# Low parts of layer 1's weights and of the first unit's work: from GpSimd to VectorE

## The chip, the cores and the metric

The kernel runs on one core of a Trainium2 chip. The metric is device time in microseconds (us) of one execution; lower is better. A core has TensorE (PE in the profile; PEld is its weight load), VectorE (DVE), ScalarE (ACT), GpSimd (POOL) and SyncE (SP), whose queue issues nearly all DMAs. Each engine runs its own list of instructions in order, and waits on semaphores where an operand comes from another engine.

## The reference

Three steps: a scan over 768 positions, then two dense layers.

```python
def _attn_ref(q, k, v, a_re, a_im):            # (4, 8, 768, 48) each
    mag = np.sqrt(a_re * a_re + a_im * a_im)
    scale = np.minimum(mag, 0.999) / (mag + 1e-06)
    a_re_n, a_im_n = (a_re * scale, a_im * scale)
    for t in range(S):
        ar, ai = (a_re_n[:, :, t, :, None], a_im_n[:, :, t, :, None])
        new_re = ar * S_re - ai * S_im
        new_im = ar * S_im + ai * S_re
        kv = np.einsum('bhd,bhe->bhde', k[:, :, t], v[:, :, t])
        S_re, S_im = (new_re + kv, new_im)
        y[:, :, t] = np.einsum('bhd,bhde->bhe', q[:, :, t], S_re)
...
def _moe_ref(x, w_in, w_out):                   # x 3072 x 384, w_in 384 x 2048
    h = np.maximum(x @ w_in, 0.0)
    return h * h @ w_out
...
def _moe2_ref(x, w_in, w_out):
    h = x @ w_in
    g = np.where(h > 0.0, h, alpha * (np.exp(np.minimum(h, 0.0)) - 1.0))
    return g @ w_out
```

## The kernel before

The scan is done in chunks of 128 positions. A *unit* is one chunk of two of the four batches, 256 tokens in all; there are 12 (NU). For each unit `E_steps` makes the decay from logarithms, an arctan and running sums (two matmuls with a triangle of ones), with Exp and Sin on ScalarE, and from it the scaled queries and keys qn and kn (`fin`, four halves each). `P_steps` then transposes them on TensorE, multiplies them (the scores), masks the product on VectorE (amat), multiplies it with v and adds the carried state. Its output x (`xev`, and `xmove`, six small DMAs) is the input of layer 1.

Layer 1 goes by *ticks* (u, j): for unit u and each of 16 blocks j of 128 hidden columns, `moe1_gemm1` makes the hidden block (nine matmuls, the *first product*) and ScalarE applies Relu, Square and a Copy; two ticks later `moe1_gemm2` multiplies with the second weight (nine matmuls, the *second product*). The matmuls take a rounded format, so each operand is split in two: a high part (a ScalarE copy into that format) and a low part (the operand less its high part, one subtraction). Three matmuls, high by high, high by low and low by high, then stand for one.

The weights come as 64-bit numbers. `load_bits` fetches block j of both weights of a layer into one of two raw buffers (384 KB each DMA), `decode` makes 32-bit numbers of it in three VectorE steps, and `split` makes the high and the low part, wh and wl. For layer 1 the low part is made on GpSimd (line 319), as is the activation's low part glo of every unit (line 656). Layer 2's are split later with the same function, on VectorE. The table `POOL` names what GpSimd does of `E_steps` by unit, its last entry serving all units from 2 on: rho is the product of line 441 that goes into the arctan, q0, q1, k0 and k1 are halves of qn and kn (line 523), lo is the low part of line 455. In every unit from 2 on GpSimd also handles a carry (lines 479 and 480).

Steps are put into ticks by the tables `E_AT`, `P_AT` and `D_AT`; unit 0, unit 1's `E_steps` and the decoding of layer 1's weights stand in the ticks before the first product. The order on each engine is then set by a scheduler that plays the program through with its own costs, so a step that moves to another engine moves others as well. What the profile's lines are: 231 and 242 are the helpers for ScalarE; 307 to 309 the three decode steps; 313 the check of the raw bits; 392 to 395 the running sums; 414, 433, 441, 442, 488, 494, 495, 515 and 523 VectorE's part of `E_steps`; 563, 570, 587 and 596 the matmuls of `P_steps`; 573, 603 and 613 VectorE's part of it; 648 and 669 the first and second products of layer 1; 709 and 737 those of layer 2.

Of the kernel before, what the change touches and what calls it, by code (L numbers as in the profile page):

```python
# [9 lines left out]
F32 = mybir.dt.float32  # L10
F32R = mybir.dt.float32r
U32 = mybir.dt.uint32
I32 = mybir.dt.int32
ACTF = mybir.ActivationFunctionType
ALU = mybir.AluOpType
# [178 lines left out]
def fast_path(  # L194
# [15 lines left out]
    nc = tc.nc  # L210
# [16 lines left out]
    vec = nc.vector  # L227
    pe = nc.tensor

    def act(out, in_, func, **kw):  # L230
        nc.scalar.activation(out=out, in_=in_, func=func, **kw)  # L231
# [12 lines left out]
    const = ctx.enter_context(tc.tile_pool(name="const", bufs=1))  # L244
# [9 lines left out]
    def bank(i):  # L254
        return psum.tile([128, 512], F32, tag=f"b{i}", name=f"b{i}")


    ident = const.tile([128, 128], F32, name="ident")
    mask = const.tile([128, 128], F32, name="mask")
    triph = const.tile([128, 128], F32, name="triph")  # L260
    maskr = const.tile([128, 128], F32R, name="maskr")
    bias_c = const.tile([128, 4], F32, name="bias_c")
    stat = const.tile([128, 3, 2 * NU], F32, name="stat")
    ratio = const.tile([128, NU], F32, name="ratio")
# [3 lines left out]
    def setup_consts():  # L268
        g = nc.gpsimd
        g.memset(mask, 1.0)  # L270
        g.affine_select(out=mask, in_=mask, pattern=[[1, 128]], base=0, channel_multiplier=-1,
                        compare_op=ALU.is_ge, fill=0.0)
        g.affine_select(out=ident, in_=mask, pattern=[[-1, 128]], base=0, channel_multiplier=1,
                        compare_op=ALU.is_ge, fill=0.0)
        g.memset(bias_c[:, 0:1], 1e-36)
        g.memset(bias_c[:, 1:2], math.log(2e-6))
        g.memset(bias_c[:, 2:3], 0.5 * math.pi)
        g.tensor_copy(out=maskr, in_=mask)
        vec.tensor_scalar(out=triph, in0=mask, scalar1=1.0 / TWO_PI, scalar2=None, op0=ALU.mult)

    b_eps, b_w, b_q = (bias_c[:, i:i + 1] for i in range(3))
# [8 lines left out]
    def load_bits(layer, j):  # L290

        raw = raw_p.tile([128, 2, 768], U32, tag="raw", name="raw", bufs=RAW_BUFS)
        for i, which in enumerate(("in", "out")):
            nc.sync.dma_start(out=raw[:, i], in_=wbits[which, layer][j * 128:(j + 1) * 128, :])
        return raw

    def words(raw):
        two = raw.rearrange("p i (f two) -> p (i f) two", two=2)
        return two[:, :, 0], two[:, :, 1]

    def decode(raw, pinned=False):

        w0, w1 = words(raw)
        t = raw_p.tile([128, 768], F32, tag="wf", name="wf")
        f = t.bitcast(U32)
        pin = tc.keep_in_program_order if pinned else (lambda x: x)
        pin(vec.tensor_scalar(out=f, in0=w0, scalar1=29, scalar2=0xC0000000, op0=ALU.logical_shift_right, op1=ALU.bitwise_xor))  # L307
        vec.scalar_tensor_tensor(out=f, in0=w1, scalar=3, in1=f, op0=ALU.logical_shift_left, op1=ALU.bitwise_xor)
        vec.scalar_tensor_tensor(out=f, in0=w1, scalar=0x80000000, in1=f, op0=ALU.bitwise_and, op1=ALU.bitwise_xor)
        return t  # L310
# [4 lines left out]
    def split(f, j, eng):  # L315
        hi = wts.tile([128, 768], F32R, tag=f"wh{j}", name=f"wh{j}")
        lo = wts.tile([128, 768], F32R, tag=f"wl{j}", name=f"wl{j}")
        act(hi, f, ACTF.Copy)
        eng.tensor_tensor(out=lo, in0=f, in1=hi.bitcast(F32), op=ALU.subtract)
        for i, which in enumerate(("in", "out")):  # L320
            wt[which, j] = tuple(w[:, i * 384:(i + 1) * 384] for w in (hi, lo))

# [35 lines left out]
    qk = {}  # L358


    POOL = [("k0", "rho"), ("q1",), ("q0", "k0", "lo")]

    def E_steps(u):

# [14 lines left out]
        def eng(op):  # L379
            return nc.gpsimd if op in POOL[min(u, 2)] else vec  # L380

# [259 lines left out]
    def moe1_gemm1(u, j):  # L641
        hp = bank(2 + j % 2)
        wh, wl = (t.rearrange("p (k f) -> p k f", k=3) for t in wt["in", j])
        x = xs[u]
        n = 0
        for kk in range(3):
            for w, hl in ((wh, 0), (wh, 1), (wl, 0)):
                pe.matmul(out=hp[:, :UT], lhsT=w[:, kk, :], rhs=x[:, kk, hl, :], start=(n == 0), stop=(n == 8))  # L648
                n += 1
        g = moe_p.tile([128, UT], F32, tag="g", name="g")  # L650
        hi = moe_p.tile([128, UT], F32R, tag="ghi", name="ghi", bufs=GB)
        lo = moe_p.tile([128, UT], F32R, tag="glo", name="glo", bufs=GB)
        act(g, hp[:, :UT], ACTF.Relu)
        act(g, g, ACTF.Square)
        act(hi, g, ACTF.Copy)
        nc.gpsimd.tensor_tensor(out=lo, in0=g, in1=hi.bitcast(F32), op=ALU.subtract)  # L656
        g1[u, j] = (hi, lo)

    def moe1_gemm2(u, j):
# [165 lines left out]

    def piece(j):
        raw = load_bits(0, j)
        return lambda: split(decode(raw, pinned=j < 8), j, nc.gpsimd)

    def later(t, f):  # L830
        box = []
# [31 lines left out]
    load(0, ("ar", "ai"))  # L863
    nc.scalar.preload_act_table_set(LN_EXP)
    setup_consts()
    vec.memset(stat, 0.0)
    vec.memset(wbad, 0)
# [7 lines left out]
    for t in range(NT1):  # L875
        j = t - (NT1 - FT)
# [101 lines left out]
```

## Time and profile before

| | |
|---|---|
| median of 3 runs | 1084.84 us (1082.99 to 1085.36) |
| profiled execution | 1084.96 us, span 1083.2 us |
| TensorE busy | 1027.3 us (95%) |
| ScalarE busy | 712.4 us (66%) |
| VectorE busy | 615.6 us (57%) |
| GpSimd busy | 316.3 us (29%) |
| DMA | 101.38 MB, mean 94 GB/s |

The profile cuts the span into 40 slices of 27 us. TensorE's busy tenths read 2, 8, 6, 8, 7 in the first five and 9 in nearly all from there on; VectorE's read 7, 8, 8, 9, 5 in the same five and 1 to 8 later. GpSimd's work ends soon after half of the span, with layer 1. A busy figure over the whole span is a mean over these stages, so the stages are to be read apart.

### The profile page before, as it was taken

The numbers are of one execution on the slowest core, as the hardware profiler recorded it, in microseconds if no ns is written. First come the engines' busy times: TensorE is split into PE (matmuls) and PEld (weight loads), VectorE is DVE, ScalarE is ACT, GpSimd is POOL, SyncE is SP. The second block draws the span as 40 slices with busy tenths as digits, with TensorE's granted clock in tenths as the row PEclk, the third lists the DMA queues.
The fourth block names the chain that finished last, engine by engine and source line by source line (L and its number), as shares of the span: only waits on it lengthen the run. The fifth ranks groups of instructions, "written<-read, shape, count | busy, mean of one in ns | idle before, by whom it ended". The sixth has DMA issues, their size and how long they took to land.

```text
span 1083.2 us, 18914 instructions
## 1 busy us (share of the span) xinstructions
PE 1027.3 (95%) x7362; PEld 961.8 (89%) x7362; DVE 615.6 (57%) x847; ACT 712.4 (66%) x1453; POOL 316.3 (29%) x299
## 2 busy tenths in 40 slices
PE   2868799999999999999999999999999999999997
PEld 1668799999999999999999999998989999999896
DVE  7889525547394745563422134888875554554543
ACT  6666478676777767776766578666666565655553
POOL 3367345454564535453534234000000000000000
PEclk9869999999999999999999999999999999999999
DMA  7655121423253432432100044667600010000000
GB/s 233 192 170 173 38 73 37 148 81 117 69 164 116 128 137 52 146 88 97 52 16 9 16 135 151 219 210 245 215 30 30 1 59 1 5 26 1 30 1 32
DMA packets 58555, 101.38 MB, mean 94 GB/s; under 512 B 20910, under 2 KB 28590, under 8 KB 58458
## 3 DMA queue, kind: packets, MB, share of 16 engines
q1 hardware_dynamic: 58362, 100.00, 28.5%
q8 instruction: 60, 0.98, 0.4%
q14 instruction: 37, 0.30, 0.1%
q10 hardware_dynamic: 96, 0.10, 0.0%
HBM read 81.92 MB, written 15.80 MB: 90 GB/s over the span
## 4 chain that ended last, share of the span: by engine, by line
PE 45%; DMA 5%; ACT 3%; issue 2%; DVE 2%; SPq 0%; ACTq 0%; DVEq 0%
PE b L737 14%; PE b L709 13%; PE b L669 7%; PE b L648 7%; DMA raw<-in_moe_w_out_dram 3%; DMA c_x<-in_a_im_dram 2%; ACT g L231 1%; PE b L570 1%; PE b L563 1%; PE b L587 1%; PE b L589 1%; ACT e L231 1%; DVE wbad L313 0%; ACT g2h L231 0%; PE b L596 0%
## 5 line engine op out<-in xcount | busy, mean ns | idle before, releaser
L231 ACT ACTIVATE g<-b 128x256 f32<-128x256 f32 (+1 forms) x288 | 127.8, 449 | 172.0 <-PE b L648 75.7
L648 PE MATMUL b<-x,wh 128*128 128x256 f32 x1152 | 228.4, 290 | 4.6 <-DVE wf L307 4.6
L656 POOL TENSOR_TENSOR glo<-g,ghi 128x256 fp32r<-128x256 f32 x192 | 167.3, 878 | 222.0 <-ACT ghi L231 159.3
L648 PEld LDWEIGHTS b<-x,wh 128*128 128x128 f32 x1152 | 185.8, 196 | 7.0 <-issue 6.7
L648 PE MATMUL b<-x,wl 128*128 128x256 f32 x576 | 166.6, 289 | 0.0
L669 PE MATMUL b<-glo,wh 128*128 128x256 f32 x576 | 162.8, 289 | 0.6 <-POOL glo L656 0.6
L669 PE MATMUL b<-ghi,wl 128*128 128x256 f32 x576 | 159.9, 284 | 0.0
L669 PE MATMUL b<-ghi,wh 128*128 128x256 f32 x576 | 154.3, 292 | 0.5 <-ACT ghi L231 0.5
L231 ACT ACTIVATE g<-g 128x256 f32<-128x256 f32 (+1 forms) x288 | 139.0, 487 | 5.5
L737 PE MATMUL b<-wh,g2h 128*128 128x384 f32 x384 | 129.4, 337 | 0.0
L737 PE MATMUL b<-wl,g2h 128*128 128x384 f32 x384 | 129.0, 336 | 0.0
L737 PE MATMUL b<-wh,g2l 128*128 128x384 f32 x384 | 125.5, 337 | 0.7 <-DVE g2l L726 0.7
L709 PE MATMUL b<-x2l,wh 128*128 128x512 f32 x288 | 113.6, 395 | 0.0
L709 PE MATMUL b<-x2h,wl 128*128 128x512 f32 x288 | 113.6, 395 | 0.0
L648 PEld LDWEIGHTS b<-x,wl 128*128 128x128 f32 x576 | 112.9, 196 | 0.2 <-issue 0.2
L669 PEld LDWEIGHTS b<-glo,wh 128*128 128x128 f32 x576 | 110.1, 191 | 2.7 <-POOL glo L656 1.4
L709 PE MATMUL b<-x2h,wh 128*128 128x512 f32 x288 | 112.1, 389 | 0.0
L669 PEld LDWEIGHTS b<-ghi,wl 128*128 128x128 f32 x576 | 110.0, 191 | 0.3 <-issue 0.2
L669 PEld LDWEIGHTS b<-ghi,wh 128*128 128x128 f32 x576 | 104.5, 192 | 2.8 <-ACT ghi L231 0.9
L726 DVE TENSOR_TENSOR g2l<-g,g2h 128x512 fp32r<-128x512 f32 x96 | 66.6, 695 | 70.4 <-ACT g2h L231 69.8
L723 DVE SCALAR_TENSOR_TENSOR g<-e,g 128x512 f32<-128x512 f32 x96 | 66.1, 690 | 61.5 <-ACT g L231 61.5
L231 ACT ACTIVATE g2h<-g 128x512 fp32r<-128x512 f32 x96 | 60.1, 627 | 57.8 <-DVE g L724 57.5
(117 smaller groups left out, 1942.6 us busy)
## 6 DMA issues: line engine op xcount, KB each, us to landing
raw<-in_moe_w_in_dram SPq DMA_DIRECT2D x48, 384.0 KB
raw<-in_moe_w_out_dram SPq DMA_DIRECT2D x48, 384.0 KB
w2d<-wf SPq DMA_DIRECT2D x16, 384.0 KB
w<-w2d SPq DMA_DIRECT2D x8, 768.0 KB
ld_ar<-in_a_re_dram SPq DMA_DIRECT2D x12, 384.0 KB
ld_ai<-in_a_im_dram SPq DMA_DIRECT2D x12, 384.0 KB
ld_q<-in_q_dram SPq DMA_DIRECT2D x12, 384.0 KB
vt<-in_v_dram SPq DMA_DIRECT2D x12, 384.0 KB
```

The costliest lines, as they stand in the source:

```text
L231: nc.scalar.activation(out=out, in_=in_, func=func, **kw)
L563: pe.transpose(ps[0:E, i * 128:(i + 1) * 128], qk[n, u, b][:, h].rearrange("p c d -> p (c d)"), ident)
L570: pe.matmul(out=ps[:, i * 128:(i + 1) * 128], lhsT=L["k", b, g][:, i * 128:(i + 1) * 128], rhs=L["q", b, g][:, i * 128:(i + 1) * 128], sta ...
L587: pe.matmul(out=o, lhsT=vv[:, gi * D:gi * D + 64], rhs=L["a", b, g][:, i, :], start=True, stop=(c == 0))
L589: pe.matmul(out=o, lhsT=st[:, gi * D:gi * D + 64], rhs=L["q", b, g][:, i * 128:(i + 1) * 128], start=False, stop=True)
L648: pe.matmul(out=hp[:, :UT], lhsT=w[:, kk, :], rhs=x[:, kk, hl, :], start=(n == 0), stop=(n == 8))
L656: nc.gpsimd.tensor_tensor(out=lo, in0=g, in1=hi.bitcast(F32), op=ALU.subtract)
L669: pe.matmul(out=acc1[u][m], lhsT=w[:, c], rhs=g, start=(j == 0 and n == 0 and m != 1), stop=(j == FT - 1 and n == 2), skip_group_check=True)
L709: pe.matmul(out=hp, lhsT=w[:, kk, :], rhs=x[:, kk], start=(i == 0), stop=(i == 8))
L723: vec.scalar_tensor_tensor(out=g, in0=e, scalar=1.0, in1=g, op0=ALU.add, op1=ALU.mult)
L726: vec.tensor_tensor(out=lo, in0=g, in1=hi.bitcast(F32), op=ALU.subtract)
L737: pe.matmul(out=acc2[n][s][:, :DM], lhsT=g[:, t], rhs=w, start=(j == 0 and i == 0), stop=(j == FT - 1 and i == 2))
```

## The change

Three edits. The low part of layer 1's weights is subtracted on VectorE (`piece` passes vec). The low part of the activation is subtracted on VectorE for unit 0 and on GpSimd, as it was, for the others. The table POOL is empty for units 0 and 1. Besides, `split` gets a branch that would make the low part with matmuls; no caller passes pe, so it is not taken, and its constant `minus` is written once. The lines of the changed kernel stand 2 to 11 higher (L307 becomes L309, L319 becomes L330, L656 becomes L667, L515 and L523 become L526 and L534).

```diff
@@ -259,6 +259,7 @@
     mask = const.tile([128, 128], F32, name="mask")
     triph = const.tile([128, 128], F32, name="triph")
     maskr = const.tile([128, 128], F32R, name="maskr")
+    minus = const.tile([128, 128], F32R, name="minus")
     bias_c = const.tile([128, 4], F32, name="bias_c")
     stat = const.tile([128, 3, 2 * NU], F32, name="stat")
     ratio = const.tile([128, NU], F32, name="ratio")
@@ -276,6 +277,7 @@
         g.memset(bias_c[:, 1:2], math.log(2e-6))
         g.memset(bias_c[:, 2:3], 0.5 * math.pi)
         g.tensor_copy(out=maskr, in_=mask)
+        g.tensor_scalar(out=minus, in0=ident, scalar1=-1.0, scalar2=None, op0=ALU.mult)
         vec.tensor_scalar(out=triph, in0=mask, scalar1=1.0 / TWO_PI, scalar2=None, op0=ALU.mult)
 
     b_eps, b_w, b_q = (bias_c[:, i:i + 1] for i in range(3))
@@ -316,7 +318,16 @@
         hi = wts.tile([128, 768], F32R, tag=f"wh{j}", name=f"wh{j}")
         lo = wts.tile([128, 768], F32R, tag=f"wl{j}", name=f"wl{j}")
         act(hi, f, ACTF.Copy)
-        eng.tensor_tensor(out=lo, in0=f, in1=hi.bitcast(F32), op=ALU.subtract)
+        if eng is pe:
+
+            for i in range(2):
+                c = slice(i * 384, i * 384 + 384)
+                ps = bank(7)
+                pe.matmul(out=ps[:, :384], lhsT=ident, rhs=f[:, c], start=True, stop=False)
+                pe.matmul(out=ps[:, :384], lhsT=minus, rhs=hi[:, c], start=False, stop=True)
+                act(lo[:, c], ps[:, :384], ACTF.Copy)
+        else:
+            eng.tensor_tensor(out=lo, in0=f, in1=hi.bitcast(F32), op=ALU.subtract)
         for i, which in enumerate(("in", "out")):
             wt[which, j] = tuple(w[:, i * 384:(i + 1) * 384] for w in (hi, lo))
 
@@ -358,7 +369,7 @@
     qk = {}
 
 
-    POOL = [("k0", "rho"), ("q1",), ("q0", "k0", "lo")]
+    POOL = [(), (), ("q0", "k0", "lo")]
 
     def E_steps(u):
 
@@ -653,7 +664,7 @@
         act(g, hp[:, :UT], ACTF.Relu)
         act(g, g, ACTF.Square)
         act(hi, g, ACTF.Copy)
-        nc.gpsimd.tensor_tensor(out=lo, in0=g, in1=hi.bitcast(F32), op=ALU.subtract)
+        (nc.gpsimd if u else vec).tensor_tensor(out=lo, in0=g, in1=hi.bitcast(F32), op=ALU.subtract)
         g1[u, j] = (hi, lo)
 
     def moe1_gemm2(u, j):
@@ -825,7 +836,7 @@
 
     def piece(j):
         raw = load_bits(0, j)
-        return lambda: split(decode(raw, pinned=j < 8), j, nc.gpsimd)
+        return lambda: split(decode(raw, pinned=j < 8), j, vec)
 
     def later(t, f):
         box = []
```

With the edits the scheduler orders other engines' work anew. On TensorE, around the transposes of unit 1 (kernel before; b2 and b3 take the first products of unit 0, wh2 is the high part of weight 2, qn0 and kn0 are unit 1's, ident is the transposes' other operand):

```order
L648 MATMUL b3_590<-x_351,wh1_190 128x256 x2
L648 MATMUL b3_590<-x_351,wl1_191 128x256
L563 MATMUL b6_705<-ident_79,qn0_607 96x128 x4
L648 MATMUL b2_613<-x_351,wh2_206 128x256 x2
L648 MATMUL b2_613<-x_351,wl2_207 128x256
L648 MATMUL b2_613<-x_351,wh2_206 128x256 x2
L648 MATMUL b2_613<-x_351,wl2_207 128x256
L648 MATMUL b2_613<-x_351,wh2_206 128x256 x2
```

And in the changed kernel, around the same transposes (b2 and b3 now hold the first products of weights 4 and 5):

```order
L659 MATMUL b2_683<-x_353,wh4_247 128x256 x2
L659 MATMUL b2_683<-x_353,wl4_248 128x256
L659 MATMUL b3_733<-x_353,wh5_309 128x256 x2
L659 MATMUL b3_733<-x_353,wl5_310 128x256
L659 MATMUL b3_733<-x_353,wh5_309 128x256 x2
L659 MATMUL b3_733<-x_353,wl5_310 128x256
L659 MATMUL b3_733<-x_353,wh5_309 128x256 x2
L659 MATMUL b3_733<-x_353,wl5_310 128x256
L680 MATMUL b0_632<-ghi_626,wh2_208 128x256
L680 MATMUL b1_633<-ghi_626,wh2_208 128x256
L574 MATMUL b6_707<-ident_79,qn0_609 96x128 x4
```

The first transpose of unit 1 stood after the first products of weights 0 and 1; now it stands after those of weights 0 to 5, the second products of weights 0 and 1 and the first two matmuls of weight 2's.

On VectorE, the end of the weights' decoding (before; wf_551 is the last of the sixteen weights, ld_q and x1 are unit 2's, raw_2351 holds layer 2's bits, amat_879 is unit 1's):

```order
L307 TENSOR_SCALAR wf_551<-raw_516 128x768
L308 SCALAR_TENSOR_TENSOR wf_551<-raw_516,wf_551 128x768
L309 SCALAR_TENSOR_TENSOR wf_551<-raw_516,wf_551 128x768
L515 TENSOR_TENSOR ld_q_829<-ld_q_829,x2_900 128x768
L515 TENSOR_TENSOR x1_831<-x1_831,x3_901 128x768
L313 SCALAR_TENSOR_TENSOR wbad_86<-raw_2351,wbad_86 128x768
L573 TENSOR_TENSOR amat_879<-b4_874,mask_80 128x512
L603 TENSOR_TENSOR st1_92<-b5_890,tcol_526 96x384
```

And now, around the same pair of unit 2 (wl13 and wl12 are low parts of the weights):

```order
L310 SCALAR_TENSOR_TENSOR wf_533<-raw_504,wf_533 128x768
L526 TENSOR_TENSOR ld_q_831<-ld_q_831,x2_902 128x768
L526 TENSOR_TENSOR x1_833<-x1_833,x3_903 128x768
L311 SCALAR_TENSOR_TENSOR wf_533<-raw_504,wf_533 128x768
L584 TENSOR_TENSOR amat_881<-b4_876,mask_80 128x512
L614 TENSOR_TENSOR st1_93<-b5_892,tcol_528 96x384
L330 TENSOR_TENSOR wl13_512<-wf_507,wh13_511 128x768
L667 TENSOR_TENSOR glo_1074<-g_1072,ghi_1073 128x256
L330 TENSOR_TENSOR wl12_538<-wf_533,wh12_537 128x768
L499 SCALAR_TENSOR_TENSOR x6_1009<-x5_781,x4_1008 128x768
L309 TENSOR_SCALAR wf_541<-raw_515 128x768
```

The pair on ld_q and x1 and unit 1's scores amat stood behind all sixteen decodes; now they stand ahead of the last two decodes and of the last four low parts, and the check of layer 2's bits is behind them.

On SP's queue, the last loads of layer 1's weights (before; td takes unit 2's exponentials to memory, tcol fetches them back):

```order
L294 DMA raw_513<-in_moe_w_in_dram 128x768
L294 DMA raw_513<-in_moe_w_out_dram 128x768
L294 DMA raw_516<-in_moe_w_in_dram 128x768
L294 DMA raw_516<-in_moe_w_out_dram 128x768
L294 DMA raw_2351<-in_moe2_w_in_dram 128x768
L294 DMA raw_2351<-in_moe2_w_out_dram 128x768
L463 DMA td_94<-x2_900 1x768
```

And now:

```order
L296 DMA raw_504<-in_moe_w_in_dram 128x768
L296 DMA raw_504<-in_moe_w_out_dram 128x768
L474 DMA td_95<-x2_902 1x768
L296 DMA raw_515<-in_moe_w_in_dram 128x768
L296 DMA raw_515<-in_moe_w_out_dram 128x768
L478 DMA tcol_909<-td_95 48x16x1 x2
L296 DMA raw_518<-in_moe_w_in_dram 128x768
L296 DMA raw_518<-in_moe_w_out_dram 128x768
```

The loads of the last two weights (raw_515 and raw_518; raw_513 and raw_516 before) went out ahead of td; now they stand behind it, and the last one behind tcol too.

## Rows read from the trace of the kernel before

**Rows 1.** Busy time by stretch: stretch, length, busy us (instructions) per engine, clock, DMA.

```profile
57.50:80.00 22.50, 16.87 (x102) 16.29 (x102) 19.78 (x20) 16.47 (x31) 16.36 (x10) 0.65 0.50 162
80.00:114.00 34.00, 24.84 (x200) 23.45 (x200) 32.51 (x26) 20.14 (x45) 24.37 (x17) 0.95 0.48 151
114.00:138.00 24.00, 22.14 (x167) 21.49 (x164) 9.21 (x16) 13.18 (x30) 8.37 (x10) 0.86 0.17 50
138.00:300.00 162.00, 161.22 (x1451) 155.38 (x1450) 83.05 (x115) 119.78 (x267) 79.11 (x72) 1.00 0.28 87
```

**Rows 2.** TensorE's waits: who waited for whom, total us, times, longest.

```profile
PE b L587 <- DVE amat L573: 7.8, 3, 4.6
PE b L563 <- DVE qn L523: 5.4, 1, 5.4
...
PE b L563 <- ACT qT L231: 3.3, 1, 3.3
PE b L563 <- POOL qn L523: 1.9, 1, 1.9
```

**Rows 3.** Timeline of TensorE: start, us, instruction, idle time before it and releaser.

```profile
57.52 0.77 PE L648 MATMUL b<-x,wh 128*128 128x256 f32 x2 [4.59 <-DVE wf L307]
...
100.51 0.33 PE L395 MATMUL b<-x,maskr 128*128 128x384 f32 x1
...
133.83 0.64 PE L563 MATMUL b<-ident,qn 128*96 128x128 f32 x4 [1.86 <-POOL qn L523]
```

**Rows 4.** Timeline of VectorE in the opening.

```profile
12.04 0.55 DVE L307 TENSOR_SCALAR wf<-raw 128x768 uint32<-128x768 uint32 x1
...
27.72 0.54 DVE L523 TENSOR_TENSOR qn<-x,ld_q 128x384 f32<-128x384 f32 x1
28.19 0.55 DVE L523 TENSOR_TENSOR kn<-x,x 128x384 f32<-128x384 f32 x1
...
48.24 0.95 DVE L515 TENSOR_TENSOR ld_q<-ld_q,x 128x768 f32<-128x768 f32 x1
49.11 0.95 DVE L515 TENSOR_TENSOR x<-x,x 128x768 f32<-128x768 f32 x1
...
54.84 0.28 DVE L613 TENSOR_TENSOR x<-b,x 128x128 fp32r<-128x128 f32 x1
55.05 0.54 DVE L495 SCALAR_TENSOR_TENSOR x<-x,b 128x384 f32<-128x384 f32 x1
...
103.12 2.49 DVE L309 SCALAR_TENSOR_TENSOR wf<-raw,wf 128x768 uint32<-128x768 uint32 x1
105.53 0.95 DVE L515 TENSOR_TENSOR ld_q<-ld_q,x 128x768 f32<-128x768 f32 x1
106.40 5.05 DVE L515 TENSOR_TENSOR x<-x,x 128x768 f32<-128x768 f32 x1
...
112.77 0.68 DVE L573 TENSOR_TENSOR amat<-b,mask 128x512 f32<-128x512 f32 x1
113.38 0.54 DVE L603 TENSOR_TENSOR st<-b,tcol 96x384 f32<-96x384 f32 x1
```

**Rows 5.** Busy time by stretch, for the list of VectorE from its first decode.

```profile
12.04:55.35 43.31, 28.02 (x143) 19.95 (x142) 39.86 (x57) 27.55 (x48) 17.38 (x9) 0.88 0.62 192
12.04:105.61 93.57, 65.98 (x408) 56.23 (x407) 85.39 (x98) 60.35 (x115) 52.33 (x31) 0.84 0.56 180
```

**Rows 6.** Timeline of GpSimd beside the long instruction of VectorE.

```profile
106.25 1.92 POOL L480 TENSOR_TENSOR x<-x,x 1x768 f32<-1x768 f32 x1 [1.46 <-ACT x L242]
108.14 1.82 POOL L319 TENSOR_TENSOR wl<-wf,wh 128x768 fp32r<-128x768 f32 x1
```

**Rows 7.** GpSimd, 0 to 138: line, operands, count, busy us, mean ns, idle before.

```profile
L319 POOL TENSOR_TENSOR wl<-wf,wh 128x768 fp32r<-128x768 f32 x16 | 34.4, 2158 | 34.2 <-ACT wh L231 32.3 <-PE b L570 1.8
L656 POOL TENSOR_TENSOR glo<-g,ghi 128x256 fp32r<-128x256 f32 x18 | 16.9, 951 | 19.5 <-ACT ghi L231 15.9 <-issue 2.9 <-POOL glo L656 0.8
```

**Rows 8.** VectorE from 138 on: layer 2's low parts of the weights.

```profile
L319 DVE TENSOR_TENSOR wl<-w,wh 128x768 fp32r<-128x768 f32 x16 | 15.7, 979 | 15.5 <-ACT wh L231 15.3
```

## The prediction

> **What bounds the kernel now.** I read the busy time by stage first. From 138 us on, TensorE is the bound: in 138 to 300 it is busy 161.22 of 162 us [rows 1]. Before that it is not: 16.87 of 22.5, 24.84 of 34 and 22.14 of 24 us in the three stretches from 57.5 on, at a granted clock of 0.65 to 0.95. What is full there is VectorE, with 19.78 of 22.5 and 32.51 of 34 us [rows 1]. So the span is a starved opening and then TensorE at its own pace, and whatever the opening gains or loses reaches the end one for one, as long as nothing behind it begins to wait.
>
> Next, who ended TensorE's waits: 7.8 us for the masked scores (amat, VectorE), 5.4 us for unit 1's qn, 3.3 us for an eviction on ScalarE, 1.9 us for unit 2's qn [rows 2]. Unit 0's first weight product starts at 57.52 [rows 3]. Then VectorE's list in order of time. From its first decode at 12.04 to the end of its sixteenth at 103.12 + 2.49 = 105.61 it holds 96 instructions. Undisturbed, one follows the next after 0.87 us (768 columns, two inputs: 48.24 to 49.11), 0.47 (384 columns, 27.72 to 28.19; the one-input decode step alike), 0.61 (the scores, 112.77 to 113.38) and 0.21 (128 columns, 54.84 to 55.05) [rows 4]. With 42, 45, 6 and 3 of each that is 62 us. The stretch lasted 93.57 us, of which VectorE was busy 85.39 [rows 5]: 8.2 us of waits and 85.4 - 62 = 23.4 us in which an instruction was running but took longer than its kind needs. The plainest case: the L515 at 106.40 took 5.05 us where its twin at 49.11 took 0.95 [rows 4], while GpSimd worked without a break from 106.25 on [rows 6]. So VectorE loses time to GpSimd, and the first unit's low parts are most of what GpSimd does there: 16 weight low parts of 2158 ns and 18 activation ones of 951 ns, 16 of them unit 0's [rows 7].
>
> The Trainium skill says the same in "SBUF — State Buffer", section "Who interferes with whom": a VectorE instruction with two SBUF inputs and a GpSimd instruction that reads SBUF exclude each other, and the later one blocks fully. The 5.05 us agree with it.
>
> **The change part by part.** *Added to VectorE.* Sixteen weight low parts: the very instruction, on VectorE for layer 2, took 979 ns in the mean [rows 8], undisturbed spacing 0.87. Sixteen activation low parts of 256 columns: no such row; between 0.21 (128 columns) and 0.47 (384), I take 0.34. Four halves of qn or kn and two of the angle product at 0.47 each. Sum: 13.9 + 5.4 + 2.8 = 22.1 us. The matmul branch in split is never taken, and the minus tile is written once on GpSimd and read by nobody: one small instruction before 3 us, nothing.
>
> *Removed.* GpSimd's copies of the same, and with them the stretching. Still on GpSimd in the opening are unit 2's carry and its low part (L480 took 1.92 [rows 6], and two more stand there that I take to be like it). At worst all 23.4 us stay, at best none; I keep 4 us, the size of the GpSimd work that is left.
>
> *The path to the last weight.* In the changed order VectorE issues 138 instructions from the first decode to the last weight's low part: 61 of 0.87, 52 of 0.47, 8 of 0.61, 14 of 0.34, 3 of 0.21, or 87.8 us. With the waits of before (8.2) and 4 of stretch it ends at 12.04 + 87.8 + 8.2 + 4 = 112.0. In the old kernel the last low part ended on GpSimd at 108.14 + 1.82 = 109.96 [rows 6]. So the weights come no sooner, and the gain must come from what TensorE has done by then.
>
> *What TensorE has done by then.* Three things move it ahead. First, the list up to unit 0's x is 52 instructions, 32.9 us; with the 3.5 us of waits of that stretch (43.31 less 39.86 busy [rows 5]) x is done near 48.5 where it was done at 54.84 + 0.28 = 55.1 [rows 4]; part of the copy that follows is issued by ScalarE behind a table load and the arctan of unit 1, so of 6.6 us I count 5: first product near 52.5. Second, the transposes of unit 1, on which TensorE stood 5.4 us, now come behind the products of weights 2 to 5, which are ready. Third, unit 1's scores stood behind the 5.05 us instruction and a check; both are out of their way. Before, TensorE at 113.4 still had to do the first products of weights 13 to 15 and six second products of unit 0. By the new order, what is left after the last low part until the same state (unit 0 done, the first two products of unit 1 done) is 45 matmuls at 0.12 us = 5.4 us, and 1 us for the last activation's way through ScalarE and VectorE: 112.0 + 6.4 = 118.4. Before, that state was reached at 133.83 - 1.86 = 131.97 [rows 3]. Difference 13.6 us. From TensorE's own side the bound is wider: 5 us of earlier start and 5.4 + 7.8 + 3.3 us of waits [rows 2], 21.5 us, so VectorE decides.
>
> *What is late next.* 38 instructions that waited on GpSimd's queue for ScalarE now wait at the head of VectorE's, with decodes and scores behind them. They mostly stand two or more instructions behind what they need; at 0.1 us each that is 4 us. At worst they would wait as long as layer 2's did, 15.5 us for 16 [rows 8], which had nothing else to do; at best nothing. SP's queue is moved too: unit 2's td now goes out ahead of the loads of the last two weights; it is priced under the rivals. The wait for unit 2's qn (1.9) I leave as it is.
>
> *Sum.* The profiled execution took 1084.96 us (span 1083.2, 1.8 around it; the median of the runs shown is 1084.84, so no correction). 1084.96 - 13.6 + 4 = 1075.4. All of it comes from the first 135 us; behind them, order and load of TensorE stay.
>
> **The rivals.**
> *VectorE overfilled (slower).* VectorE is the fullest engine of the stretch and gets 22 us more. If its long instructions are long for another reason than GpSimd (so the 23.4 us stay), the last low part ends at 12.04 + 87.8 + 8.2 + 23.4 = 131.4, the state at 137.8, 5.8 us later than before, with the 4 us of waits: 1094.8. It turns from gain to loss once more than 4 + 9.6 = 13.6 of the 23.4 us stay. For it: how full VectorE is [rows 1]. Against: the 5.05 us [rows 4, 6].
> The Trainium skill's "Perfetto Trace Analysis", section "Optimizing Scalar/DVE Operations", would side with this rival: where VectorE is saturated it advises moving work off it, even to GpSimd, though it adds that the two share a port and that this might not help. By its advice this change goes the wrong way; by its caveat it is open.
>
> *A ring of waits (no difference).* Unit 2's L515 pair needs exponentials of sums that TensorE makes behind the product of weight 11. Before, it stood behind all sixteen decodes; now it stands ahead of the last low parts of weights 12 to 15, and td with it ahead of two loads. VectorE gets there near 12.04 + 72.7 + 8.2 + 4 = 97. In the old trace those sums ended at 100.51 + 0.33 = 100.84 and the pair began at 105.53 [rows 3, 4], 4.7 later. To be in time the sums must end near 92.3, 8.5 us sooner. TensorE's 5 us and 5.4 us just cover that. If they don't come, VectorE stands up to 8.5 us here, and the result is 1075.4 + 8.5 = 1083.9.
>
> *More than forecast.* No stretch left, no new wait, and the wait for unit 2's qn gone: 1075.4 - 4 - 4 - 1.9 = 1065.5. It needs everything in step.
>
> **How the numbers follow.** Forecast 0.66, more 0.08, ring 0.13, overfilled 0.13. The forecast's own range is 1069 to 1082 (stretch and waits each from 0 to 8 us, the ring half paid). To hold 8 in 10 I go from 1067 to 1087, which takes in the ring and the mild half of the overfilled case. About 0.2% (2.2 us) is what a measurement of this kernel tells from no change. Faster: forecast, more, and a quarter of the ring, 0.77; within: most of the ring, 0.10; slower: 0.13.
>
> **What would show it.** In the new profile, decode steps and qn products before 70 us should run at 0.55 and 0.95 us with no long ones, GpSimd should be almost empty until unit 2; VectorE should still be over 90% busy until about 112; the first product near 52.5, the last low part near 112, unit 2's first transpose near 120. I am wrong if long VectorE instructions remain where GpSimd is idle, if VectorE's waits in the opening go well over 12 us, if unit 2's L515 pair waits for ScalarE by several us, or if TensorE gains waits behind 138 us.

## The result and the profile after

| | before | after |
|---|---|---|
| median | 1085.1 us (1082.99 to 1086.5) | 1068.03 us (1065.6 to 1070.96) |
| profiled execution | 1084.96 us | 1065.77 us, span 1064.0 us |
| GpSimd busy, 10 to 110 us | 57.4 us | 7.2 us |
| GpSimd busy, whole span | 316.3 us | 255.5 us |
| VectorE busy, whole span | 615.6 us | 611.5 us |

The ratio is 0.9844, 95% interval 0.9817 to 0.9871: 17 us faster, 7 us more than the forecast of 1075.4. In a later set of runs the changed kernel took 1070.4 us (1066.51 to 1073.2, ratio 0.9847, 0.9823 to 0.9872). VectorE has 885 instructions where it had 847, and is busy for less time in all.

The gain is made in the opening and then carried: unit 0's output (x2s, line 685 after) starts 17.1 us earlier, the last unit's 17.9 and the last output of layer 2 19.2 us earlier (1055.82 against 1075.02). Busy time by stretch of the kernel after, in the columns of [rows 1]; the first row is the same stretch of the kernel before cut shorter, for the clock:

```profile
57.50:70.00 12.50, 7.05 (x32) 6.78 (x33) 11.95 (x13) 7.89 (x14) 7.71 (x5) 0.50 0.41 134
```

```profile
57.50:80.00 22.50, 21.25 (x172) 19.78 (x174) 22.50 (x36) 21.36 (x46) 2.12 (x1) 1.00 0.46 152
80.00:114.00 34.00, 29.74 (x253) 27.96 (x252) 31.29 (x49) 20.61 (x45) 5.11 (x2) 1.00 0.54 174
114.00:138.00 24.00, 21.68 (x186) 20.43 (x185) 9.53 (x16) 20.07 (x44) 12.65 (x13) 0.93 0.26 84
138.00:300.00 162.00, 161.60 (x1449) 156.43 (x1447) 92.56 (x124) 118.53 (x262) 78.64 (x72) 1.00 0.33 100
57.50:70.00 12.50, 11.25 (x87) 10.21 (x88) 12.50 (x23) 11.96 (x26) 0.00 (x0) 1.00 0.47 155
```

In 57.5 to 80 TensorE does 172 matmuls where it did 102 [rows 1]. Part of that is its clock: in 57.5 to 70 it was granted 0.50 before (1.2 GHz), behind the 4.59 us in which it stood [rows 3], and 1.00 after (2.4 GHz). GpSimd goes from 16.36 to 2.12 us in the first stretch, and VectorE runs 36 instructions in 22.5 us where it ran 20 in 19.78. From 138 us on TensorE was and is the bound.

VectorE's list of the opening after, beside [rows 5]: from its first decode to the end of the sixteenth it now holds 133 instructions instead of 96 (the row counts two more that only overlap its ends, as [rows 5] does).

```profile
11.87:103.45 91.58, 71.09 (x512) 60.54 (x511) 87.86 (x135) 65.31 (x129) 7.23 (x3) 0.89 0.57 176
```

By the undisturbed spacings of the prediction the 133 need 84.9 us. VectorE was idle for 91.58 - 87.86 = 3.7 us of the list, so 87.9 - 84.9 = 3.0 us of stretch are left of 23.4. How VectorE's lines ran in 12 to 100 us, first before, then after (line, operation, operands, count, busy us, mean ns, idle before):

```profile
L309 DVE SCALAR_TENSOR_TENSOR wf<-raw,wf 128x768 uint32<-128x768 uint32 x14 | 16.5, 1186 | 0.1
...
L523 DVE TENSOR_TENSOR kn<-x,x 128x384 f32<-128x384 f32 x6 | 5.8, 987 | 0.5 <-ACT x L242 0.5
...
L573 DVE TENSOR_TENSOR amat<-b,mask 128x512 f32<-128x512 f32 x6 | 4.1, 684 | 1.2 <-PE b L570 1.2
```

```profile
L311 DVE SCALAR_TENSOR_TENSOR wf<-raw,wf 128x768 uint32<-128x768 uint32 x14 | 13.2, 950 | 0.1
...
L584 DVE TENSOR_TENSOR amat<-b,mask 128x512 f32<-128x512 f32 x8 | 5.4, 681 | 0.0
...
L534 DVE TENSOR_TENSOR kn<-x,x 128x384 f32<-128x384 f32 x8 | 4.4, 548 | 0.0
```

The decode's third step fell from 1186 to 950 ns and kn from 987 to 548, with the same operands. The scores amat did not move (684, 681): one of their inputs, b, is a bank of PSUM, the memory that TensorE writes to, and not of SBUF, where the other operands lie.

TensorE's steps after, beside [rows 3], and VectorE's around unit 0's x, unit 2's pair and the last low part, beside [rows 4]:

```profile
51.93 0.77 PE L659 MATMUL b<-x,wh 128*128 128x256 f32 x2 [3.20 <-DMA x<-x]
...
88.83 0.34 PE L406 MATMUL b<-x,maskr 128*128 128x384 f32 x1
...
114.10 0.28 PE L659 MATMUL b<-x,wl 128*128 128x256 f32 x1
...
118.02 1.09 PE L574 MATMUL b<-ident,qn 128*96 128x128 f32 x4 [0.98 <-POOL qn L534]
```

```profile
46.45 0.28 DVE L624 TENSOR_TENSOR x<-b,x 128x128 fp32r<-128x128 f32 x1
...
90.72 0.95 DVE L526 TENSOR_TENSOR ld_q<-ld_q,x 128x768 f32<-128x768 f32 x1
91.59 0.95 DVE L526 TENSOR_TENSOR x<-x,x 128x768 f32<-128x768 f32 x1
...
105.46 0.95 DVE L330 TENSOR_TENSOR wl<-wf,wh 128x768 fp32r<-128x768 f32 x1
```

The sums that the ring of waits hung on end at 89.17, and unit 2's pair follows at 90.72 without a wait. The second of the pair, 5.05 us long before [rows 4], takes 0.95. "Unit 0 done, first two products of unit 1 done" is reached at 114.10 + 0.28 = 114.38; before, at 131.97. TensorE's waits after, beside [rows 2]:

```profile
PE b L574 <- DVE qn L534: 4.2, 2, 3.7
...
PE b L598 <- DVE amat L584: 2.3, 1, 2.3
```

Waiting for amat fell from 7.8 to 2.3 us; the wait for unit 2's qn from 1.86 to 0.98.

### The profile page after: what moved, and what is told of

Same layout as the page of the kernel before. It is cut to its first block, busy times and chain, and to the rows that moved or that the text cites. A ratio compares the mean times of both kernels' runs of the same rounds, so it can differ in the third digit from the quotient of the medians.

```text
span 1064.0 us, 18892 instructions
## 1 busy us (share of the span) xinstructions
PE 1019.2 (96%) x7362; PEld 954.4 (90%) x7362; DVE 611.5 (57%) x885; ACT 711.8 (67%) x1453; POOL 255.5 (24%) x262
## 4 chain that ended last, share of the span: by engine, by line
PE 83%; issue 3%; DVE 2%; DMA 1%; POOL 1%; ACT 1%; SPq 0%; ACTq 0%; DVEq 0%; POOLq 0%
PE b L748 19%; PE b L720 19%; PE b L680 16%; PE b L659 16%; PE b L581 3%; PE b L574 3%; PE b L598 2%; PE b L607 2%; PE b L600 2%; DMA raw<-in_moe_w_out_dram 1%; PE b L405 1%; DVE x L526 1%; PE b L406 1%; ACT x L242 0%; POOL qn L534 0%
## 5 line engine op out<-in xcount | busy, mean ns | idle before, releaser
L659 PE MATMUL b<-x,wh 128*128 128x256 f32 x1152 | 225.5, 288 | 6.4 <-DMA x<-x 3.8
L667 POOL TENSOR_TENSOR glo<-g,ghi 128x256 fp32r<-128x256 f32 x176 | 146.3, 837 | 212.3 <-ACT ghi L231 146.8
L659 PEld LDWEIGHTS b<-x,wh 128*128 128x128 f32 x1152 | 182.1, 192 | 9.5 <-DVE wf L310 3.3
L659 PE MATMUL b<-x,wl 128*128 128x256 f32 x576 | 164.1, 285 | 0.0
L659 PEld LDWEIGHTS b<-x,wl 128*128 128x128 f32 x576 | 110.6, 192 | 0.3 <-issue 0.3
L231 ACT ACTIVATE g2h<-g 128x512 fp32r<-128x512 f32 x96 | 60.1, 627 | 57.7 <-DVE g L735 57.5
```

The lines of the kernel that those rows point to most:

```text
L667: (nc.gpsimd if u else vec).tensor_tensor(out=lo, in0=g, in1=hi.bitcast(F32), op=ALU.subtract)
```

## The experiments

The theory: GpSimd's reads of the first unit's operands stretched VectorE's instructions, and the change gains because they are gone. Rivals: the gain comes from the new order of the engines, from unit 0's x alone, or from one of the three edits by itself. Each run was timed beside the kernel before on its chip. Of the code, only lines that differ are shown, and not those that put the scratch tile dumo in the place of minus. *Stretch* is VectorE's busy time in its list, from the first decode to the end of the sixteenth, less the undisturbed spacings.

**GpSimd's reading put back (gp_back).** The changed kernel; beside each weight GpSimd makes four subtractions that nobody needs, on columns of that weight's high part. In the trace VectorE's, ScalarE's and SP's order is that of the changed kernel instruction by instruction, and TensorE's too, but for one of its 7362 matmuls, which comes nine places later.

```diff
-        return lambda: split(decode(raw, pinned=j < 8), j, vec)
+        def work():
+            split(decode(raw, pinned=j < 8), j, vec)
+            for w in (wt["in", j][0], wt["out", j][0]):
+                for c in (w[:, 0:192], w[:, 192:384]):
+                    nc.gpsimd.tensor_tensor(out=dumo, in0=c.bitcast(F32), in1=c.bitcast(F32), op=ALU.subtract)
+        return work
```

> The changed kernel with idle work put back on GpSimd: for each of layer 1's sixteen weights four subtractions of 192 columns that read the high part and write a scratch tile nobody reads. VectorE, ScalarE and SyncE get the same lists in the same order as in the changed kernel. If GpSimd's reading is what stretches VectorE's instructions, the stretch of VectorE's list up to the last low part goes from about 3 us to 12 or more, that low part from 106 to 114 or later, and the time to 1074 to 1084. If the gain comes from the new order alone, all stays: low part at 106 to 107, time 1066 to 1071.

Measured: 1078.13 us (1077.53 to 1078.46), ratio 0.993 (0.9914 to 0.9947): 10 us over the changed kernel. The stretch of the list rose from 3.0 to 14.5 us, its waits fell to 2.0, and the sixteenth decode ended at 113.37 instead of 103.45. VectorE's timeline in this run, and GpSimd's beside it:

```profile
94.10 1.26 DVE L309 SCALAR_TENSOR_TENSOR wf<-raw,wf 128x768 uint32<-128x768 uint32 x1
...
97.60 0.94 DVE L309 SCALAR_TENSOR_TENSOR wf<-raw,wf 128x768 uint32<-128x768 uint32 x1
...
101.07 0.68 DVE L583 TENSOR_TENSOR amat<-b,mask 128x512 f32<-128x512 f32 x1
...
104.22 1.26 DVE L329 TENSOR_TENSOR wl<-wf,wh 128x768 fp32r<-128x768 f32 x1
```

```profile
92.10 3.62 POOL L843 TENSOR_TENSOR dumo<-wh 128x192 f32<-128x192 f32 x4 [1.84 <-ACT wh L231]
100.96 1.87 POOL L490 TENSOR_TENSOR x<-x,x 1x768 f32<-1x768 f32 x1 [5.24 <-ACT x L242]
102.80 7.55 POOL L843 TENSOR_TENSOR dumo<-wh 128x192 f32<-128x192 f32 x8
```

One and the same decode step takes 1.26 us beside GpSimd's subtractions (to 95.72) and 0.94 while GpSimd idles (to 100.96). With the order held, GpSimd's reading costs 10 us. That shows the theory for the changed kernel. What was put back is not the same work as what was taken away (69.0 us of GpSimd in the list here, 52.3 before), so the 10 us are not the exact share of the 17.

**What of GpSimd's work does it (gp_write, gp_one).** In place of the four subtractions GpSimd writes constants, after a copy of 16 columns that ties it to the same moment; or it copies (one input).

```diff
+            nc.gpsimd.tensor_copy(out=dumo[:, 0:16], in_=c[:, 0:16])
+            for i in range(20):
+                nc.gpsimd.memset(dumo, 1.0)
```

> The changed kernel, and for each of the sixteen weights GpSimd copies 16 columns and then writes a constant 20 times into a scratch tile of 192 columns, reading nothing. Theory (VectorE is held up by what GpSimd reads): VectorE's list keeps a stretch of 2 to 4 us, time 1066 to 1071. Rival (any work of GpSimd that touches the memory holds VectorE up, by as much as it is busy): stretch 10 us or more, time 1075 to 1080 as with the 64 subtractions (1078.13).

```diff
+                for c in (w[:, 0:192], w[:, 192:384]) * 2:
+                    nc.gpsimd.tensor_copy(out=dumo, in_=c.bitcast(F32))
```

> The changed kernel, and for each of the sixteen weights GpSimd copies 192 columns of its high part eight times into a scratch tile (one input, half a microsecond each by guess, 128 copies). Theory (VectorE is held up by what GpSimd reads, one input or two): VectorE's two-input instructions grow long beside the copies, stretch 6 to 15 us, time 1071 to 1079. Rival (only two-input instructions of GpSimd hold VectorE up): stretch 2 to 4 us, time 1066 to 1071.

Measured: gp_write 1070.41 us (1068.51 to 1079.75), ratio 0.9882 (0.9844 to 0.992), against 1070.4 of the changed kernel in the same set; stretch 5.4 us. gp_one 1079.91 us (1077.43 to 1084.38), ratio 0.995 (0.9932 to 0.9968); stretch 10.4. GpSimd's and VectorE's lines in 12 to 100 us, gp_write first, then gp_one, and between them two instructions of gp_write's timeline, each with the one of GpSimd beside it:

```profile
L844 POOL MEMSET dumo<- 128x192 f32 x200 | 55.9, 279 | 11.4
L329 DVE TENSOR_TENSOR wl<-wf,wh 128x768 fp32r<-128x768 f32 x14 | 13.3, 949 | 0.1
L310 DVE SCALAR_TENSOR_TENSOR wf<-raw,wf 128x768 uint32<-128x768 uint32 x14 | 16.5, 1182 | 0.1
```

```profile
81.78 2.59 DVE L310 SCALAR_TENSOR_TENSOR wf<-raw,wf 128x768 uint32<-128x768 uint32 x1
81.55 2.01 POOL L465 TENSOR_TENSOR x<-x,x 128x768 fp32r<-128x768 f32 x1
...
93.02 2.57 DVE L310 SCALAR_TENSOR_TENSOR wf<-raw,wf 128x768 uint32<-128x768 uint32 x1
92.66 2.11 POOL L490 TENSOR_TENSOR x<-x,x 1x768 f32<-1x768 f32 x1 [0.63 <-ACT x L242]
```

```profile
L843 POOL COPY dumo<-wh 128x192 f32<-128x192 f32 x77 | 57.0, 741 | 24.2 <-ACT wh L231 19.7
L329 DVE TENSOR_TENSOR wl<-wf,wh 128x768 fp32r<-128x768 f32 x12 | 12.2, 1016 | 0.4 <-ACT wh L231 0.3
L310 DVE SCALAR_TENSOR_TENSOR wf<-raw,wf 128x768 uint32<-128x768 uint32 x14 | 15.5, 1116 | 0.1
```

GpSimd is as busy in both (55.9 and 57.0 us of such work), but only the reading costs time that shows in the medians. The medians are 9.5 us apart. 5.0 of them come in the opening (17.4 against 12.4 us gained, in the table below), as much as the stretches differ. The rest comes later, where gp_one's order is another: from 97 us on 27 of VectorE's 885 places hold another instruction. gp_write's VectorE runs in the unchanged order, and TensorE's and ScalarE's order departs only from 124 us on. What is left of its 5.4 us stands mostly beside GpSimd's reads for unit 2, which the changed kernel has too: the long instructions among the fourteen of L310 are the two shown, and the others took 0.94 to 0.96 us. The Trainium skill states this in "SBUF — State Buffer", section "Who interferes with whom": an instruction of VectorE with two SBUF inputs contends with one of GpSimd that reads SBUF and not with one that only writes it, and with at most one SBUF input it does not contend, unless it runs in one of the modes that use two ports. These runs agree on two inputs (1.26 against 0.94 us beside reads, 949 ns beside writes) and on amat with its PSUM input (0.68 us). The decode's first step, which has one SBUF input, was held as well: 1.72 us at 83.78 in the changed kernel beside a GpSimd read, where it takes 0.55 undisturbed. Whether it runs in such a mode no run shows.

**One edit alone (w_only, glo_only, table_only), and all but one (no_weights, no_glo, no_table).** The first three are the kernel before with one of the changed lines (the + lines below), the other three the changed kernel with one of them put back (the - lines):

```diff
 w_only, no_weights:
-        return lambda: split(decode(raw, pinned=j < 8), j, nc.gpsimd)
+        return lambda: split(decode(raw, pinned=j < 8), j, vec)
 glo_only, no_glo:
-        nc.gpsimd.tensor_tensor(out=lo, in0=g, in1=hi.bitcast(F32), op=ALU.subtract)
+        (nc.gpsimd if u else vec).tensor_tensor(out=lo, in0=g, in1=hi.bitcast(F32), op=ALU.subtract)
 table_only, no_table:
-    POOL = [("k0", "rho"), ("q1",), ("q0", "k0", "lo")]
+    POOL = [(), (), ("q0", "k0", "lo")]
```

> The kernel before with only the weights' low parts on VectorE. They are 34.4 of about 58 us of GpSimd's work in the opening. If the stretching is what was lost, this part alone removes over half of the 23 us of stretch for 13.9 us of added work, and gives 5 to 11 us: 1074 to 1080. If the new order is what counts, it depends on whether unit 1's first transposes move behind the products of weights 2 to 5; where they stay, no more than 3 us: 1082 to 1085.

> The kernel before with only unit 0's sixteen activation low parts on VectorE. They take about 15 us of GpSimd from 69 us on. By the stretching: some 6 us of stretch go for 5.4 us of added work, and the second products no longer wait behind weights in GpSimd's queue: 2 to 5 us, 1080 to 1083. If the shorter way of the activation to the second product were the main cause, 8 us or more: 1077 or less.

> The kernel before with only the table of GpSimd's steps emptied for units 0 and 1: six instructions of 384 columns move to VectorE, 7 us of GpSimd for 2.8 us of VectorE. By the stretching: 0 to 3 us, 1082 to 1085. If the start of the chain of units 0 and 1 were the main cause, unit 0's first product comes 4 us sooner and the time is 1080 or less.

> The changed kernel with the weights' low parts back on GpSimd (unit 0's activation low parts and the emptied table stay). If the parts simply add, by the runs that did one alone (weights -4.4, activation +2.2, table -7.9 against the kernel before): 1085.5 - 7.9 + 2.2 = 1080. If emptying GpSimd is what lets the others work, more is lost than 4.4 from the changed kernel's 1068: 1076 or more either way; the stretch of VectorE's list should be back at 15 us or more.

> The changed kernel with unit 0's activation low parts back on GpSimd. If the parts add, this is better than the changed kernel by 2.2: 1066. If the last GpSimd work in the opening matters by its reading, 15 us of it bring some 6 us of stretch back and second products wait again: 1071 to 1075.

> The changed kernel with the table of GpSimd's steps as it was before for units 0 and 1. If the parts add: 1068 + 7.9 = 1076, and unit 0's x is late again, near 54 instead of 46.7. If the table gave its 7.9 only because it relieved a full GpSimd queue, which is empty here, the loss is below 3: 1068 to 1071.

Then, since the table alone gained without less stretch, the table for unit 0 alone:

```diff
-    POOL = [("k0", "rho"), ("q1",), ("q0", "k0", "lo")]
+    POOL = [(), ("q1",), ("q0", "k0", "lo")]
```

> The kernel before with the table emptied for unit 0 alone (its halves of kn and its angle product on VectorE, unit 1's q1 still on GpSimd). If the table's 7.9 us come from the start of unit 0's chain: x near 48.5 as in the run with both, and 1077 to 1080. If they come from unit 1's qn no longer standing behind weights on GpSimd: 1082 to 1086.

All results, with TensorE's progress, which is the number of its matmuls in the profile from 0 to 140 us and from 140 to 200. The kernel before has 626 and 535. A difference in matmuls, times 0.12 us (one follows the next after that at full clock, 113.03 to 113.15 after), is the time gained on the kernel before in that part; an estimate, since not all matmuls are equally long.

| run | median us | ratio (95%) | stretch us | x of unit 0 | matmuls 0 to 140 | 140 to 200 | gained, us: opening, 140 to 200 |
|---|---|---|---|---|---|---|---|
| after | 1068.03 | 0.9844 (0.9817, 0.9871) | 3.0 | 46.73 | 785 | 532 | 19.1, -0.4 |
| after_again | 1070.4 | 0.9847 (0.9823, 0.9872) | 3.4 | 46.24 | 775 | 532 | 17.9, -0.4 |
| gp_write | 1070.41 | 0.9882 (0.9844, 0.992) | 5.4 | 46.01 | 771 | 530 | 17.4, -0.6 |
| gp_back | 1078.13 | 0.993 (0.9914, 0.9947) | 14.5 | 48.66 | 702 | 531 | 9.1, -0.5 |
| gp_one | 1079.91 | 0.995 (0.9932, 0.9968) | 10.4 | 47.31 | 729 | 502 | 12.4, -4.0 |
| w_only | 1081.13 | 0.9956 (0.9939, 0.9973) | 6.9 | 54.09 | 720 | 481 | 11.3, -6.5 |
| glo_only | 1087.73 | 1.0016 (1.0005, 1.0026) | 20.5 | 55.23 | 638 | 488 | 1.4, -5.6 |
| table_only | 1077.64 | 0.9923 (0.9905, 0.9941) | 24.0 | 48.54 | 700 | 546 | 8.9, 1.3 |
| no_weights | 1084.11 | 0.9989 (0.9975, 1.0003) | 21.9 | 48.66 | 694 | 481 | 8.2, -6.5 |
| no_glo | 1085.08 | 0.9994 (0.9973, 1.0015) | 8.9 | 46.47 | 678 | 481 | 6.2, -6.5 |
| no_table | 1072.51 | 0.9875 (0.9857, 0.9894) | 7.5 | 54.60 | 745 | 515 | 14.3, -2.4 |
| table_u0 | 1084.25 | 1.0000 (0.9985, 1.0015) | 25.2 | 48.49 | 701 | 476 | 9.0, -7.1 |
| b_more | 1075.95 | 0.9902 (0.9887, 0.9917) | 3.4 | 46.78 | 767 | 474 | 16.9, -7.3 |

Against what was expected: gp_back and after_again came as forecast, gp_write in its time but with more stretch (5.4 for 2 to 4), gp_one 0.9 us over its range. no_weights came as its second forecast had it, table_only, table_u0 and b_more (below) as their rivals had it, though in table_u0 x came as early as the theory said. The times of w_only and no_table lie between their two forecasts, those of glo_only and no_glo above both.

By their times the edits do not add: alone they gain 4.4, -2.2 and 7.9 us, 10 of 17, and leaving out the weights or glo loses all of it. The progress columns take this apart. The two of a row add up to the gain in the medians within 2.4 us in every row. In the opening the edits alone gain 11.3 + 1.4 + 8.9 = 21.6 us, against 19.1 together. What breaks the sum of the single edits is 140 to 200 us, where w_only, glo_only, no_weights, no_glo and table_u0 lose 5.6 to 7.1 us (no_table and gp_one lose 2.4 and 4.0; why stays open). There TensorE changes over to unit 2. With one edit left out, the opening does not add either: without glo it gains 6.2 of 19.1 us, though glo alone was worth 1.4. The end of this part says why. Busy time in that stretch, first table_u0, then after:

```profile
175.00:190.00 15.00, 11.97 (x86) 10.38 (x86) 10.66 (x15) 8.49 (x17) 5.78 (x4) 0.89 0.64 222
185.00:190.00 5.00, 5.00 (x37) 4.58 (x37) 2.12 (x3) 1.06 (x2) 0.00 (x0) 0.66 0.79 286
```

```profile
175.00:190.00 15.00, 15.00 (x136) 14.69 (x137) 11.42 (x15) 10.89 (x24) 8.30 (x7) 1.00 0.65 212
185.00:190.00 5.00, 5.00 (x44) 5.00 (x43) 3.19 (x5) 3.02 (x7) 2.90 (x3) 1.00 0.14 4
```

What happens there, in the timelines of VectorE, TensorE and SP of table_u0, and of SP after:

```profile
179.34 0.28 DVE L613 TENSOR_TENSOR x<-b,x 128x128 fp32r<-128x128 f32 x1
```

```profile
184.77 0.50 PE L648 MATMUL b<-x,wh 128*128 128x256 f32 x2 [2.17 <-DMA x<-x]
```

```profile
178.45 0.35 SPq L344 DMA_DIRECT2D ld_ar<-in_a_re_dram  x1
178.86 0.42 SPq L344 DMA_DIRECT2D x<-in_k_dram  x1
179.45 0.33 SPq L344 DMA_DIRECT2D ld_ai<-in_a_im_dram  x1
179.87 3.68 SPq L621 DMA_DIRECT2D x<-x  x6
```

```profile
167.02 3.68 SPq L632 DMA_DIRECT2D x<-x  x6
170.81 0.53 SPq L355 DMA_DIRECT2D ld_ar<-in_a_re_dram  x1
```

The last step of unit 2's x starts at 179.34 (166.71 after, 174.16 in table_only). Its copies land five microseconds later, TensorE stands 2.17 us, and then runs 185 to 190 at a granted clock of 0.66: 86 matmuls in 15 us against 136. In no_weights the same three things stand at 180.13, 2.22 us and 0.66.

The copies are late because of what stands ahead of them on SP's queue. In table_u0 three loads for a later unit go out just before the six copies, and the DMA moves 324 GB/s in the 4 us behind x; after, the loads stand behind the copies, and it is 40. That holds in all runs: in just these five the loads stand ahead, and unit 2's first product starts 4.8 to 6.0 us behind the end of x, after waits of 1.8 to 3.0 us. In every other run they stand behind, and it starts 2.7 to 4.0 us behind x with no wait for the copies. TensorE's order is not what differs: in the kernel before, in no_table and in the five, x ends behind the same 1029 matmuls and its first use is the same 1053rd.

So these five runs pay at the change to unit 2, because each edit also makes the scheduler place the loads anew. No run moved the loads alone, so the cause is argued from all runs and not shown by an experiment.

The table (table_only) is worth its 8.9 us of the opening without less stretch (24.0): unit 0's x comes at 48.5 instead of 55.1, since its chain no longer passes through GpSimd's halves of kn and its product for the angle. table_u0, with the table emptied for unit 0 alone, has the same x and gains the same 9.0 us there. "Less stretch" is thus not the whole of the gain. gp_back, with the reading put back and the table empty, keeps 9.1 us of the opening's 19.1. So roughly half came with the reading, and the other half is what the table brings alone.

In no_glo the collision is seen from the other side. GpSimd's timeline, and TensorE's:

```profile
67.06 6.27 POOL L667 TENSOR_TENSOR glo<-g,ghi 128x256 fp32r<-128x256 f32 x2 [3.98 <-ACT ghi L231]
```

```profile
72.69 0.58 PE L680 MATMUL b<-glo,wh 128*128 128x256 f32 x1 [4.42 <-POOL glo L667]
```

Two small subtractions, 951 ns each in the mean before [rows 7], take 6.27 us on GpSimd, and TensorE waits 4.42 us for them. The first takes 5.58 of it, until VectorE, which meanwhile ran eight instructions back to back at their undisturbed spacing, stops at 72.06. Here GpSimd is the one that is held.

**One step further (b_more), beside the changed kernel once more (after_again).**

```diff
-    POOL = [(), (), ("q0", "k0", "lo")]
+    POOL = [(), (), (), ("q0", "k0", "lo")]
-            return nc.gpsimd if op in POOL[min(u, 2)] else vec
+            return nc.gpsimd if op in POOL[min(u, 3)] else vec
-        (nc.gpsimd if u else vec).tensor_tensor(out=lo, in0=g, in1=hi.bitcast(F32), op=ALU.subtract)
+        (nc.gpsimd if u > 1 else vec).tensor_tensor(out=lo, in0=g, in1=hi.bitcast(F32), op=ALU.subtract)
```

> The changed kernel once more, to stand on the same chip as the runs beside it: 1068 us within 3 (1065.6 to 1071.0 were measured before).

> The changed kernel, with the table POOL empty for unit 2 too and the activation's low parts of unit 1 on VectorE too. Theory (what GpSimd still reads in the opening costs VectorE time, and TensorE waits 0.98 us for unit 2's qn): the list has under 2.5 us of stretch, the wait for qn goes, time 1064 to 1068, at least 1 us under the changed kernel. Rival (the opening is emptied of GpSimd already; more work on VectorE only makes units 1 and 2 late): TensorE waits 2 to 8 us for x of units 1 and 2 between 118 and 200 us, time 1070 to 1076.

Measured: 1075.95 us (1074.82 to 1076.57) against 1070.4 of the changed kernel: the rival. The stretch did not fall (3.4 in both), nor did the wait for unit 2's qn (0.93 us). Beside after_again, the opening loses 1 us by progress and the change to unit 2 another 7. There VectorE is the late one; its busy time is 10.00 of 10 us in 170 to 180. TensorE's timeline in b_more, and the stretches (columns of [rows 1]):

```profile
174.15 0.64 PE L574 MATMUL b<-ident,kn 128*96 128x128 f32 x4 [3.25 <-DVE x L624]
```

```profile
170.00:175.00 5.00, 1.54 (x12) 1.04 (x11) 5.00 (x9) 4.23 (x8) 1.96 (x1) 1.00 0.33 132
175.00:180.00 5.00, 4.52 (x21) 4.49 (x22) 5.00 (x6) 1.86 (x3) 2.01 (x1) 0.51 0.33 77
```

This speaks for the boundary of the change: behind unit 0, in the order that came out, VectorE had no room for this. Its two parts were not tried apart, and the order moved here too.

## Why the prediction was right, point by point

*What bounds the opening.* Right: VectorE was the full engine, it was stretched by GpSimd's reads, and TensorE's gain there reached the end (17.6 us at the state named, 17 to 19 at the end).

*The stretch that stays, forecast 4 us:* 3.0. Right, and gp_back shows the cause. The four instructions of the list that still ran long all stand beside GpSimd's three for unit 2, and none where GpSimd is idle. The plainest case of the prediction, 5.05 us, is more than one delay: it ran beside four instructions of GpSimd in a row, the two of [rows 6] and the two of this line (kernel before):

```profile
109.92 2.11 POOL L656 TENSOR_TENSOR glo<-g,ghi 128x256 fp32r<-128x256 f32 x2
```

*Unit 0's x, forecast 48.5, first product 52.5:* 46.73 and 51.93. Right: the list held the 52 instructions counted, with waits of 1.4 us where 3.5 were allowed. The table is what brings it (48.5 in table_only, 54.6 in no_table).

*The path to the last weight, forecast 112.0:* 105.46 + 0.95 = 106.41. The work was as counted. The waits were not: I carried over the old 8.2 us, and there were 3.7 in the list. The old list's waits in part stood for what was moved: 1.8 us for GpSimd's low part and 2.0 for a raw buffer, which became 0 and 0.7. Of the 5.6 us between forecast and trace, 4.5 are these waits, about 1 the smaller stretch.

*New waits, forecast 4 us:* none that a view shows. VectorE's lines up to 114 us, after:

```profile
L330 DVE TENSOR_TENSOR wl<-wf,wh 128x768 fp32r<-128x768 f32 x16 | 15.7, 984 | 0.1
...
L667 DVE TENSOR_TENSOR glo<-g,ghi 128x256 fp32r<-128x256 f32 x16 | 6.4, 413 | 0.0
```

The sixteen low parts of the weights waited 0.1 us in all, those of the activation not at all: VectorE's other work filled the time between.

*From the last low part to the state, forecast 6.4 us:* 114.38 - 106.41 = 8.0. Too short by 1.6.

*TensorE's clock,* priced at nothing, was half as fast in 57.5 to 70 before as after. It is inside the difference at the state, since I worked from VectorE's path; from TensorE's side I would have missed it.

Together: 5.6 us from the last low part, 4 from the waits that did not come, less 1.6, make 8.0 of the 9.6 us between the forecast and the profiled execution; of the other 1.6, 0.9 is the shorter wait for unit 2's qn, the rest is open. The step that was mis-sized is the waits: 12.2 us allowed (8.2 + 4), 3.7 measured. The time came out near the lower end of the stated range (1067) for this reason.

*The rivals.* VectorE overfilled did not come: 3.0 us stayed, where more than 13.6 would have turned it. The ring did not come: the sums ended at 89.17, not later than the 92.3 it needed. "More than forecast" (1065.5, chance 0.08) is what nearly came: no new wait, 3.0 us of stretch where it had none, and 0.98 us left of the wait for unit 2's qn. The Trainium skill's advice in "Perfetto Trace Analysis", section "Optimizing Scalar/DVE Operations", to move work off a saturated VectorE, even to GpSimd, describes the kernel before, the slower one by 17 us; its caveat, that the two share a port and the move might not help, is what the runs bear out.

*What I did not see:* that unit 2's x was in time only by the order that came out on SP's queue. The forecast says that behind the opening order and load of TensorE stay, and it follows SP's queue only up to the weights' last loads. In five of the part-runs the loads went ahead of x's copies, and those runs lost 5.6 to 7.1 us there. The prediction had no step for it; that it was spared is luck.

## What to carry to other kernels

Work on GpSimd that reads SBUF is not free beside a full VectorE: price it by what it takes from VectorE's instructions, those with two SBUF inputs above all, and by what it loses to them itself. When a starved opening is made faster, look next at where the following unit's input is due and at what stands ahead of it on the DMA queue. A gap there costs its length, and in four of these five runs some microseconds at a lower clock as well. When a scheduler orders the work, parts tried one by one measure the order as well; hold the order and put the suspected cost back.

## What the runs showed of the hardware

- GpSimd's added work in VectorE's list, and the stretch above the changed kernel's 3.0: two-input reads 61.9 us busy and 11.6 us (gp_back); one-input copies 66.6 and 7.4 (gp_one); constant writes with small copies 68.8 and 2.4 (gp_write), of which about 2.0 stand beside unit 2's reads. As an estimate from these, a microsecond of GpSimd's reading took 0.11 to 0.19 us from VectorE.
- Being held is a matter of single instructions, and one of them can wait through several of the other engine's: beside 192-column reads a 0.94 us step of VectorE took 1.26; beside four instructions of GpSimd in a row the L515 of [rows 4] took 5.05; beside eight of VectorE in a row one subtraction of GpSimd took 5.58 (no_glo), 0.95 in the mean before.
- At the change to unit 2, after TensorE stood 1.8 to 3.25 us, its granted clock fell for some microseconds in five runs (0.66 over five microseconds in table_u0, no_weights and glo_only, 0.51 in b_more, 0.77 and then 0.89 in no_glo), and not in w_only, where it stood longest of the part-runs (2.97 us, then 1.00).
- Six small copies of unit 2's x landed within 2.7 to 4.0 us of x where no three loads stood just ahead of them on SP's queue, and 4.8 to 6.0 us behind x where they did.
